# Router search of a mixture-of-experts layer: 6-bit digits and two token chunks per set of mask columns instead of 7-bit digits

## The chip, the cores and the metric

The kernel runs on one core of a Trainium2 chip. The metric is the device time in microseconds (us) of that core. The profile's names for the engines: PE is TensorE (matrix multiply), PEld its weight loads, DVE is VectorE, ACT ScalarE, POOL GpSimd, SP SyncE (which issues most DMA). Engine names with a q are their sequencers.

## The reference

Three stages follow each other: attention with a tanh cap, a dense feed-forward layer with squared ReLU, and a mixture of 8 experts whose assignment is greedy and global:

```
N, D, E, F = 1792, 768, 8, 1024;  cap = N // E          # 224 tokens per expert
logits = x @ w_gate                                      # [1792, 8]
order = argsort(-logits.flatten())                       # best (token, expert) pair first
for idx in order:
    tok, e = idx // E, idx % E
    if assigned[tok] >= 0 or counts[e] >= cap: continue
    assigned[tok] = e; counts[e] += 1
for e in range(E):
    out[assigned == e] = relu(x[assigned == e] @ w1[e]) @ w2[e]
```

Every expert ends with exactly 224 tokens. The kernel doesn't sort. It works in 8 rounds ("routes"). In a round every free token takes its best expert that still has room; the round ends at the logit at which the first expert becomes full; what lies above it is assigned, and that expert is closed.

## The kernel before

**Stages.** Attention of four batches is interleaved with the first layer (`hidden` and `output`, matmuls of 128x128 weights against 448 tokens, each value as a high and a low part, so three matmuls a product: lines 400 to 402 and 457 to 459). From about 600 us on the class method `second` runs two things against each other: the main stream (`output(NB-1)`, `output(LAST)`, then `expert(0)` to `expert(7)`) and the side stream (the last logits, then the routes 0 to 7 and, for each, `listed`, which turns the chosen tokens into row indices for a gather).

**The order of the work.** The order on PE is written by the program (`manual_schedule`). Every step of a stream is a `yield` that adds a planned time to a clock `te`. After each piece of the main stream, a side step is put in as soon as its planned wait is over. These waits are the table `START, MASK, VOTE, REST, GATHER, LIST` (line 45); its first numbers hold until the experts begin, its second ones afterwards (`self.late`). They decide how many main matmuls stand between a route's step on DVE and the matmul that reads its result. PE works strictly in that order: a matmul whose operand isn't ready holds up all behind it. DVE's order comes from a scheduler that ranks route steps and evictions ahead; DVE, too, works in order.

**A route's search.** The 14 token chunks (`TC`) lie as 128 partitions x 14 columns. `m` is each token's best logit and `B` its one-hot expert. The logit's bits are made into a sortable 32-bit key. The threshold at which the first expert is full is searched in digits of `BITS` = 7 bits, so `NDIG` = 5 digits and `NV` = 128 possible values of a digit. A digit works like this:

1. `compare` (L626, DVE): mask[token, value, chunk] = value <= digit of the token, 128x1792 bf16.
2. The vote (L661, PE): for each of the 14 chunks one 128x128 weight load of the mask and one matmul with that chunk's `B` (8 columns), summed in PSUM: how many tokens of each expert lie at or above each value. One more matmul (L662) with a one-row operand takes off the free places (`nroom`).
3. L664 and L665 (DVE): the maximum over the experts, then `>= 0`: P says which values are still full enough.
4. L668 (PE): a matmul of P with ones (`p1`) counts them and spreads the count over all partitions.
5. L671 (DVE): the next digit `D` of every token, from `up` (L657), `p1` and the digits prepared before.

After the digits come the exact ranks: `tm`, then matmuls L682, L684, L689, L690, L703 with DVE steps between, and the rooms are updated. `listed` compares slot numbers with the values 0 to 127 (L738), multiplies (L742, 14 loads and matmuls of 4 columns), and gathers token rows by POOL (L764); `feed` transposes them on PE (L783). The experts' matmuls are L848 (first layer, experts 0 to 3, plain fp32), L855 (experts 4 to 7, split into parts) and L894 (second layer). ACT and DVE split each 128x768 weight tile into its parts (L357, L358), DVE also finishes the evictions of the experts' hidden layer (L866). `finish` transposes an output tile of the layer before (L435) and stores it (L437, L438); the gather of the last two of the six tiles can start only when the last one is stored.

Of the kernel before, what the change touches and what calls it, by code (L numbers as in the profile page):

```python
# [16 lines left out]
OP = mybir.AluOpType  # L17
AX = mybir.AxisListType
# [3 lines left out]
NE, F2 = 8, 1024  # L22
# [22 lines left out]
START, MASK, VOTE, REST, GATHER, LIST = (7.7, 11.0), (2.31, 4.2), (0.9, 3.2), (0.86, 2.6), (11.0, 12.4), (6.0, 16.0)


def shape_constants():
    p = np.arange(128)
    parts, cols = [], {}  # L50

    def add(name, a):
        a = np.asarray(a, np.float32)
        if a.shape[0] < 128:
            a = np.concatenate([a, np.zeros((128 - a.shape[0], a.shape[1]), np.float32)])
        o = sum(x.shape[1] for x in parts)
        cols[name] = (o, o + a.shape[1])
        parts.append(a)

    e = np.arange(NE)  # L60
    add("ident", np.eye(128))
    add("rev", np.tile(8.0 - e, (128, 1)))
    add("first", np.tile(224.0 * e + 1, (128, 1)))
    add("shift", np.tile(BITS * np.arange(NDIG)[::-1], (128, 1)))
    nf = sum(x.shape[1] for x in parts)
    add("tri", p[:, None] < p[None, :])
    c1, e1 = np.divmod(np.arange(TC * NE), NE)
    g2, r2 = np.divmod(np.arange(2 * TC * NE), TC * NE)
    c2, e2 = np.divmod(r2, NE)
    same = e1[:, None] == e2[None]  # L70
    add("above", same * np.where(g2[None] == 0, c1[:, None] < c2[None], True))
    add("tied", same * np.where(g2[None] == 0, False, c1[:, None] < c2[None]))
    add("val", np.tile(np.arange(NV), (128, 1)))
    add("tok", np.stack([np.tile(np.arange(TC), (128, 1)), np.tile(p[:, None], (1, TC))], 2).reshape(128, 2 * TC))
    return np.concatenate(parts, 1), cols, nf

# [4 lines left out]
class Kernel:  # L81
# [485 lines left out]
    def router_setup(self):  # L567
        nc, rp = self.nc, self.rp
        nb = CONSTS.shape[1] - NFC
        tmp = self.wts.tile([128, DM], I64, name="raw", bufs=3).bitcast(F32)[:, :nb]  # L570
        nc.sync.dma_start(tmp, self.cst[:, NFC:])
        self.cb = rp.tile([128, nb], BF, name="cb", bufs=1)
        nc.vector.tensor_copy(self.cb, tmp)
        self.k = lambda n: self.cb[:, COLS[n][0] - NFC:COLS[n][1] - NFC]
        self.tok = self.k("tok").rearrange("p (c k) -> p c k", k=2)
        self.thr = rp.tile([128, NV, TC], BF, name="thr", bufs=1)
        nc.vector.tensor_copy(self.thr, self.k("val")[:, :, None].to_broadcast([128, NV, TC]))
        self.shift = rp.tile([128, NDIG], I32, name="shift", bufs=1)
        nc.vector.tensor_copy(self.shift, self.c("shift"))
        self.unit = rp.tile([128, 2, 128], BF, name="unit", bufs=1)  # L580
        nc.vector.memset(self.unit[:, 0], 1.0)
        nc.vector.memset(self.unit[:, 1], float(NV))
        self.room = rp.tile([128, NE], F32, name="room", bufs=1)
        nc.vector.memset(self.room, float(CAP))
        self.base = rp.tile([128, NE], F32, name="base", bufs=1)
        nc.vector.tensor_copy(self.base, self.c("first"))
        self.todo = rp.tile([128, NE], F32, name="todo", bufs=1)
        nc.vector.memset(self.todo, 1.0)
        self.slot = rp.tile([128, TC], F32, name="slot", bufs=1)
        nc.vector.memset(self.slot, 0.0)  # L590
        self.spacer = rp.tile([1, 1], F32, name="spacer", bufs=1)
        self.full, self.picked, self.rows, self.xe, self.scatters = {}, {}, {}, {}, []
        self.fed = self.gathered = 0
        self.eseq = [(k, m, j) for k in range(NE) for m in (1, 2) for j in range(NF2)]
        self.eloaded = self.eready = self.esplit = 0
        self.ew = {}

    def route(self, k):


        nc, rp, v = self.nc, self.rp, self.nc.vector

        def T(shape, dt, name, bufs=1):
            return rp.tile(shape, dt, name=name, bufs=bufs)
# [7 lines left out]
        v.tensor_reduce(m, self.L, axis=AX.X, op=OP.max)  # L612
        g2 = T([128, 2, TC], F32, "g2")
        B = T([128, TC, NE], BF, "B")

        def choose():
            eo, mx = T([128, TC, NE], F32, "eo"), T([128, TC], F32, "mx")
# [4 lines left out]
            v.tensor_tensor(B, eo, mx[:, :, None].to_broadcast([128, TC, NE]), op=OP.is_equal)  # L622

        def compare(D):
            mask = T([128, NV, TC], BF, "mask")
            v.tensor_tensor(mask, self.thr, D[:, None, :].to_broadcast([128, NV, TC]), op=OP.is_le)  # L626
            return mask

        if k == NE - 1:
            choose()  # L630
            v.memset(g2[:, 0], 1.0)
            v.memset(g2[:, 1], 0.0)
            yield START[self.late], 0.0
        else:
            sg, key = T([128, TC], I32, "sg"), T([128, TC], I32, "key")
            v.tensor_scalar(sg, m.bitcast(I32), 31, -2 ** 31, op0=OP.arith_shift_right, op1=OP.bitwise_or)
            v.tensor_tensor(key, m.bitcast(I32), sg, op=OP.bitwise_xor)
            D0 = T([128, TC], I32, "D0")
            v.tensor_scalar(D0, key, BITS * (NDIG - 1), None, op0=OP.logical_shift_right)
            D = T([128, TC], BF, "D", 2)  # L640
            v.tensor_copy(D, D0)
            mask = compare(D)
            choose()
            nroom = T([1, NE], BF, "nroom")
            v.scalar_tensor_tensor(nroom, self.todo[0:1], 1.0, self.room[0:1], op0=OP.subtract, op1=OP.subtract)
            di, dig = T([128, NDIG, TC], I32, "di"), T([128, NDIG, TC], F32, "dig")
            v.tensor_tensor(di, key[:, None, :].to_broadcast([128, NDIG, TC]),
                            self.shift[:, :, None].to_broadcast([128, NDIG, TC]), op=OP.logical_shift_right)
            v.tensor_scalar(di, di, NV - 1, None, op0=OP.bitwise_and)
            v.tensor_scalar(dig, di, float(NV), None, op0=OP.add)  # L650
            yield START[self.late], 0.0
            for j in range(NDIG):
                if j:
                    mask = compare(D)
                if j < NDIG - 1:
                    up = T([128, TC], F32, "up")
                    v.tensor_scalar(up, D, float(NV), None, op0=OP.mult)  # L657
                yield MASK[self.late], 0.0
                ps = self.psum.tile([NV, NE], F32, name="aux")
                for c in range(TC):  # L660
                    nc.tensor.matmul(ps, mask[:, :, c], B[:, c], start=(c == 0), stop=False)  # L661
                nc.tensor.matmul(ps, self.unit[0:1, 0, :NV], nroom, start=False, stop=True)  # L662
                pm, P = T([NV, 1], F32, "pm"), T([NV, 1], BF, "P")
                v.tensor_reduce(pm, ps, axis=AX.X, op=OP.max)  # L664
                v.tensor_scalar(P, pm, 0.0, None, op0=OP.is_ge)  # L665
                yield VOTE[self.late], 0.4
                p1 = self.psum.tile([128, 1], F32, name="aux")
                nc.tensor.matmul(p1, self.unit[:NV, int(j < NDIG - 1)], P, start=True, stop=True)  # L668
                if j < NDIG - 1:
                    D = T([128, TC], BF, "D", 2)  # L670
                    v.scalar_tensor_tensor(D, up, p1, dig[:, j + 1], op0=OP.subtract, op1=OP.add)  # L671
                else:
                    for g, op in ((0, OP.is_gt), (1, OP.is_equal)):
                        v.tensor_scalar(g2[:, g], D, p1, -1.0, op0=OP.subtract, op1=op)
                yield 0.0, 0.1
        tm = T([128, 2, TC, NE], BF, "tm")
        v.tensor_tensor(tm, B[:, None].to_broadcast([128, 2, TC, NE]),
# [42 lines left out]
    def listed(self, k, es):  # L720

        nc, v = self.nc, self.nc.vector

        def T(shape, dt, name, bufs=1):
            return self.rp.tile(shape, dt, name=name, bufs=bufs)
# [7 lines left out]
        r = T([128, TC], BF, "r")  # L733
        v.scalar_tensor_tensor(r, half[:, :, 1], -float(TP), rel, op0=OP.mult, op1=OP.add)
        v.tensor_tensor(tk, self.tok[:, :, None, :].to_broadcast([128, TC, 2, 2]),
                        half[:, :, :, None].to_broadcast([128, TC, 2, 2]), op=OP.mult)
        oh = T([128, NV, TC], BF, "oh")
        self.picks = v.tensor_tensor(oh, self.thr, r[:, None, :].to_broadcast([128, NV, TC]), op=OP.is_equal)  # L738
        yield LIST[self.late], 0.0
        pi = self.psum.tile([128, 2, 2], F32, name="aux")  # L740
        for c in range(TC):
# [227 lines left out]
```

## Time and profile before

| quantity | value |
|---|---|
| median of 3 runs | 1083.48 us (1083.37 to 1084.87) |
| the profiled execution's own time | 1083.31 us |
| its span | 1081.5 us |
| PE busy | 1054.3 us, 97% of the span |
| DVE, ACT, POOL busy | 594.1 (55%), 470.0 (43%), 247.4 (23%) us |
| votes (35 digits x 14) | 490 matmuls, L661 |

A row of a timeline gives start, duration, engine, line, operation and tiles; where several instructions were merged, the duration is of all and the count stands at the end. Matmuls overlap on PE, so what one costs there is read from the distance between starts, not from its duration.

### The profile page before, as it was taken

Reading aid. Unit: us, or ns where it says so; the run is one execution under the profiler, and the core shown is the slowest. Engines: PE = TensorE matmul, PEld = TensorE weight load, DVE = VectorE, ACT = ScalarE, POOL = GpSimd, SP = SyncE. Lnnn points to the kernel's source line nnn. Section 1 sums busy time; section 2 is a strip of 40 time slices with the busy share of each in tenths; the row PEclk is TensorE's granted clock in tenths of the full one; section 3 lists DMA queues with packets and bytes.
Section 4 is the critical chain, followed back from the end, with each engine's and each line's share of the span. In section 5 each row is a group of like instructions: output and inputs, shape, how many; then the busy total and the mean of one; then the engine's idle time right before and its main releaser. Section 6 shows DMA issues by size and latency. Waiting matters only on the chain.

```text
span 1081.5 us, 15930 instructions
## 1 busy us (share of the span) xinstructions
PE 1054.3 (97%) x5866; PEld 833.7 (77%) x5866; DVE 594.1 (55%) x1066; ACT 470.0 (43%) x725; POOL 247.4 (23%) x181
## 2 busy tenths in 40 slices
PE   6899999999999999999999999999999999999997
PEld 2336656777677677677887888888899999999996
DVE  5997999997222145465411244444546354676550
ACT  5867686544554633454543100002232222454551
POOL 0217684764221322221000100001320201011000
PEclk9999999999999999999999999999999999999999
DMA  8744777899655599987885458567466257556620
GB/s 284 244 139 149 254 265 260 244 325 328 215 182 172 159 301 311 357 290 275 301 301 168 135 171 271 176 191 236 148 238 242 81 182 263 202 195 207 220 78 26
DMA packets 102494, 237.54 MB, mean 220 GB/s; under 512 B 11088, under 2 KB 21872, under 8 KB 102416
## 3 DMA queue, kind: packets, MB, share of 16 engines
q1 hardware_dynamic: 87776, 219.58, 60.4%
q0 software_dynamic: 3424, 11.19, 3.4%
q10 hardware_dynamic: 11216, 5.75, 2.0%
q8 instruction: 46, 0.75, 0.3%
q14 instruction: 32, 0.26, 0.1%
HBM read 194.01 MB, written 42.47 MB: 219 GB/s over the span
## 4 chain that ended last, share of the span: by engine, by line
PE 77%; issue 11%; DVE 6%; DMA 2%; ACT 1%; POOL 1%; SPq 0%; POOLq 0%; DVEq 0%; ACTq 0%
PE acc L457 8%; PE big L894 8%; PE acc L459 7%; PE acc L458 7%; PE acc L400 7%; PE acc L401 6%; PE acc L402 6%; PE acc L848 5%; PE big L234 4%; PE aux L259 4%; PE aux L661 3%; PE acc L855 2%; PE aux L267 2%; DVE wf L330 1%; PE aux L262 1%
## 5 line engine op out<-in xcount | busy, mean ns | idle before, releaser
L457 PE MATMUL acc<-g,wh 128*128 128x448 f32 x384 | 150.6, 392 | 0.0
L400 PE MATMUL acc<-xh,wh 128*128 128x448 f32 x384 | 148.0, 388 | 0.7 <-ACT r L407 0.7
L401 PE MATMUL acc<-xl,wh 128*128 128x448 f32 x384 | 140.9, 367 | 0.8 <-DVE xl L317 0.8
L459 PE MATMUL acc<-g,wl 128*128 128x448 f32 x384 | 139.8, 364 | 0.0
L458 PE MATMUL acc<-g,wh 128*128 128x448 f32 x384 | 139.8, 364 | 0.0
L402 PE MATMUL acc<-xh,wl 128*128 128x448 f32 x384 | 139.8, 364 | 0.0
L894 PE MATMUL big<-wh,g 128*112 128x384 f32 x512 | 118.2, 343 | 0.0
L238 ACT ACTIVATE p<-big,isc 128x896 f32<-128x896 f32 x96 | 85.9, 909 | 43.3 <-PE big L234 39.4
L270 DVE RECIPROCAL z<-z 128x448 f32<-128x448 f32 x24 | 70.7, 2948 | 58.5 <-ACT z L269 58.4
L412 DVE TENSOR_TENSOR g<-r,g 128x448 fp32r<-128x448 f32 x58 | 43.0, 741 | 103.2 <-ACT g L411 102.9
L400 PEld LDWEIGHTS acc<-xh,wh 128*128 128x128 f32 x384 | 71.7, 187 | 34.0 <-issue 14.7
L764 POOL DMA_INDIRECT xg<-x,idx x32 | 34.8, 1087 | 250.1 <-issue 155.0
L239 ACT ACTIVATE p<-p,capt 128x896 f32<-128x896 f32 x96 | 89.4, 948 | 1.5
L894 PEld LDWEIGHTS big<-wh,g 128*112 128x112 f32 x512 | 86.4, 175 | 0.8
L457 PEld LDWEIGHTS acc<-g,wh 128*128 128x128 f32 x384 | 72.4, 189 | 14.3 <-issue 9.6
L234 PE MATMUL big<-qk 64*128 64x448 f32 x288 | 74.5, 601 | 7.0 <-DMA qk<-qk 6.2
L401 PEld LDWEIGHTS acc<-xl,wh 128*128 128x128 f32 x384 | 72.4, 189 | 11.3 <-issue 4.6
L407 ACT ACTIVATE r<-acc 128x448 f32<-128x448 f32 x64 | 34.7, 543 | 100.9 <-PE acc L402 87.6
L402 PEld LDWEIGHTS acc<-xh,wl 128*128 128x128 f32 x384 | 72.2, 188 | 6.8 <-issue 0.8
L459 PEld LDWEIGHTS acc<-g,wl 128*128 128x128 f32 x384 | 72.0, 187 | 6.7 <-issue 0.2
L458 PEld LDWEIGHTS acc<-g,wh 128*128 128x128 f32 x384 | 72.3, 188 | 5.9 <-issue 1.7
L329 DVE TENSOR_SCALAR wf<-raw 128x512 int32<-128x512 int32 (+1 forms) x64 | 49.7, 789 | 48.7 <-DMA raw<-w_out_t 40.1
(179 smaller groups left out, 1865.4 us busy)
## 6 DMA issues: line engine op xcount, KB each, us to landing
g<-w SPq DMA_DIRECT2D x62, 384.0 KB, 6.5
wh<-wih SPq DMA_DIRECT2D x48, 384.0 KB, 4.4
wl<-wil SPq DMA_DIRECT2D x48, 384.0 KB, 4.8
wh<-woh SPq DMA_DIRECT2D x72, 256.0 KB, 2.7
wl<-wol SPq DMA_DIRECT2D x72, 256.0 KB, 3.0
wf<-w SPq DMA_DIRECT2D x33, 384.0 KB, 3.5
raw<-w SPq DMA_DIRECT2D x33, 384.0 KB, 4.3
raw<-w_in SPq DMA_DIRECT2D x16, 768.0 KB, 5.2
```

Source lines behind the costliest of these rows:

```text
L234: nc.tensor.matmul(ps[:, s, :S], k[rows], q[rows], start=True, stop=True)
L238: nc.scalar.activation(p, ps[:, :n, :S], AF.Tanh, scale=self.isc)
L239: e = nc.scalar.activation(p, p, AF.Exp, scale=self.capt)
L270: nc.vector.reciprocal(d, d)
L400: nc.tensor.matmul(ps, wh[:, d], xh, start=(d == 0), stop=False)
L401: nc.tensor.matmul(ps, wh[:, d], xl, start=False, stop=False)
L402: nc.tensor.matmul(ps, wl[:, d], xh, start=False, stop=(d == ND - 1))
L457: nc.tensor.matmul(ps, a, gh, start=(f == 0), stop=False)
L458: nc.tensor.matmul(ps, a, gl, start=False, stop=False)
L459: nc.tensor.matmul(ps, z, gh, start=False, stop=(f == NF - 1))
L848: nc.tensor.matmul(H[j], W[j][0][:, d], xs[:, d, 0].bitcast(F32), start=(d == 0), stop=(d == ND - 1))
L894: nc.tensor.matmul(acc[h][:, s, :DM // 2], l, r[:, s * (DM // 2):(s + 1) * (DM // 2)], start=(j == 0 and first), stop=(j == NF2 - 1 and last))
```

## The change

The digits become 6 bits wide: 6 digits, 64 values. The 128 mask columns of a weight load now hold 64 values for each of two halves of the tokens (`CB` = 2: chunks 0 to 6 and 7 to 13), so that a vote takes 7 matmuls of 16 columns, of which half of each result is used: rows 0 to 63 with the first half's 8 columns, rows 64 to 127 with the second's. The free places (`need`) are now taken off on DVE. Three DVE steps read a vote: `left` = need minus the first half's counts, `ge` = second half's counts >= left, and the maximum over the experts into a vote tile of 128 rows of which the upper 64 stay zero. A chunk row of mask, thresholds and digit is padded from 7 to 8 columns, which makes the mask 128x1024. `slots` takes the place of `thr` in `listed`. Six numbers of the table of waits change.

```
-BITS = 7
+BITS = 6
 NDIG = -(-32 // BITS)
 NV = 2 ** BITS
+CB = 128 // NV
+CP = TC // CB
+CQ = CP + CP % 2
+NS = 128
-START, MASK, VOTE, REST, GATHER, LIST = (7.7, 11.0), (2.31, 4.2), (0.9, 3.2), (0.86, 2.6), (11.0, 12.4), (6.0, 16.0)
+START, MASK, VOTE, REST, GATHER, LIST = (7.7, 8.0), (1.85, 3.4), (1.0, 2.6), (0.86, 2.2), (11.0, 12.4), (6.0, 10.0)
...
+        self.slots = rp.tile([128, NS, TC], BF, name="slots", bufs=1)
+        self.thr = rp.tile([128, CB * NV, CQ], BF, name="thr", bufs=1)
+        self.digit = [rp.tile([128, CB, CQ], BF, name=f"digit{i}", bufs=1) for i in range(2)]
+        self.votes = [rp.tile([128, 1], BF, name=f"votes{i}", bufs=1) for i in range(2)]
+        for d in self.digit + self.votes:
+            nc.vector.memset(d, 0.0)
...
-            mask = T([128, NV, TC], BF, "mask")
-            v.tensor_tensor(mask, self.thr, D[:, None, :].to_broadcast([128, NV, TC]), op=OP.is_le)
+            mask = T([128, CB * NV, CQ], BF, "mask")
+            v.tensor_tensor(mask.rearrange("p (a v) b -> p a v b", a=CB), self.thr.rearrange("p (a v) b -> p a v b", a=CB),
+                            D[:, :, None, :].to_broadcast([128, CB, NV, CQ]), op=OP.is_le)
...
-            nroom = T([1, NE], BF, "nroom")
-            v.scalar_tensor_tensor(nroom, self.todo[0:1], 1.0, self.room[0:1], op0=OP.subtract, op1=OP.subtract)
+            need = T([NV, NE], F32, "need")
+            v.scalar_tensor_tensor(need, self.room[:NV], 1.0, self.todo[:NV], op0=OP.add, op1=OP.subtract)
...
-                ps = self.psum.tile([NV, NE], F32, name="aux")
-                for c in range(TC):
-                    nc.tensor.matmul(ps, mask[:, :, c], B[:, c], start=(c == 0), stop=False)
-                nc.tensor.matmul(ps, self.unit[0:1, 0, :NV], nroom, start=False, stop=True)
-                pm, P = T([NV, 1], F32, "pm"), T([NV, 1], BF, "P")
-                v.tensor_reduce(pm, ps, axis=AX.X, op=OP.max)
-                v.tensor_scalar(P, pm, 0.0, None, op0=OP.is_ge)
-                yield VOTE[self.late], 0.4
+                ps = self.psum.tile([128, CB, NE], F32, name="aux")
+                for c in range(CP):
+                    nc.tensor.matmul(ps, mask[:, :, c], pairs[:, :, c], start=(c == 0), stop=(c == CP - 1))
+                ge, P = T([NV, NE], BF, "ge"), self.votes[j % 2]
+                left = need
+                for a in range(CB - 1):
+                    more = T([NV, NE], F32, f"left{a}")
+                    v.tensor_tensor(more, left, ps[a * NV:(a + 1) * NV, a], op=OP.subtract)
+                    left = more
+                v.tensor_tensor(ge, ps[(CB - 1) * NV:, CB - 1], left, op=OP.is_ge)
+                v.tensor_reduce(P[:NV], ge, axis=AX.X, op=OP.max)
+                yield VOTE[self.late], 0.45
                 p1 = self.psum.tile([128, 1], F32, name="aux")
-                nc.tensor.matmul(p1, self.unit[:NV, int(j < NDIG - 1)], P, start=True, stop=True)
+                nc.tensor.matmul(p1, self.unit[:, int(j < NDIG - 1)], P, start=True, stop=True)
...
-        self.picks = v.tensor_tensor(oh, self.thr, r[:, None, :].to_broadcast([128, NV, TC]), op=OP.is_equal)
+        self.picks = v.tensor_tensor(oh, self.slots, r[:, None, :].to_broadcast([128, NS, TC]), op=OP.is_equal)
```

The matmuls that move stand in the changed order as follows; lines of the changed kernel are 5 to 20 higher (L435 is L440 there, L661 is L677, L668 is L688, L848 is L868, L358 is L363, L783 is L803). Order rows give line, operation, output and inputs; one row of a plain fp32 matmul (L848) stands for two in the profile.

First place: PE while the fifth of the last six output tiles is transposed, in route 3. Before, from one digit's count (L668) to the next vote (L661):

```order
L668 LDWEIGHTS unit
L668 MATMUL aux<-P,unit 128x1
L457 MATMUL acc<-g,wh 128x448
L458 MATMUL acc<-g,wh 128x448
L459 MATMUL acc<-g,wl 128x448
L457 MATMUL acc<-g,wh 128x448
L458 MATMUL acc<-g,wh 128x448
L459 MATMUL acc<-g,wl 128x448
L435 MATMUL aux<-cf,xt 112x128 x4
L661 LDWEIGHTS mask
```

In the changed kernel, in the second digit of route 3:

```order
L688 LDWEIGHTS unit
L688 MATMUL aux<-votes_4841,unit 128x1
L440 MATMUL aux<-cf,xt 112x128 x4
L677 LDWEIGHTS mask
L677 MATMUL aux<-B,mask 128x16
```

Six layer matmuls that stood between the count and the transposes are gone from there; only the four transposes remain between a count and the next vote.

Second place: PE after the transposes of the sixth and last output tile, up to the first transposes of gathered rows (xg). Before, the transposes were followed by one matmul set of `listed` (14 x L742), 12 rows of L848 and a vote, which ends like this:

```order
L662 LDWEIGHTS unit
L662 MATMUL aux<-nroom,unit 128x8
L848 MATMUL big<-xs,raw 128x224 x8
L668 LDWEIGHTS unit
L668 MATMUL aux<-P,unit 128x1
L783 MATMUL aux<-cf,xg_6830 128x112
```

In the changed kernel, from the transposes on:

```order
L440 MATMUL aux<-cf,xt 112x128 x4
L868 MATMUL acc<-xs,wf 128x224 x2
L688 LDWEIGHTS unit
L688 MATMUL aux<-votes_4841,unit 128x1
L868 MATMUL acc<-xs,wf 128x224 x2
L868 MATMUL big<-xs,wf 128x224 x4
L868 MATMUL big<-xs,raw 128x224 x2
L702 LDWEIGHTS cb
L702 MATMUL aux<-tm,cb 128x224
L704 LDWEIGHTS tm
L704 MATMUL aux<-unit,tm 112x1
```

After that stand 6 and 4 more rows of L868 with the route's closing matmuls between them, then the transposes of xg. The L848 rows between the last output transposes and xg are 20 before and 20 now; the vote and the 14 matmuls of `listed` are no longer among them, the closing matmuls of route 3 are.

Third place: DVE in route 4, beside expert 0 (wl is the low part of an expert's weight tile). Before, a digit from its mask to the next:

```order
L626 TENSOR_TENSOR mask<-thr,D 128x1792
L657 TENSOR_SCALAR up<-D 128x14
L664 TENSOR_REDUCE pm<-aux 128x1
L665 TENSOR_SCALAR P<-pm 128x1
L358 TENSOR_TENSOR wl<-wf,wh 128x768 x2
L671 SCALAR_TENSOR_TENSOR D<-up,aux,dig 128x14
L358 TENSOR_TENSOR wl<-wf,wh 128x768
```

In the changed kernel:

```order
L641 TENSOR_TENSOR mask<-thr,digit_4839 128x1024
L673 TENSOR_SCALAR up<-digit_4839 128x14
L363 TENSOR_TENSOR wl<-wf,wh 128x768
L682 TENSOR_TENSOR left_7001<-need,aux 64x8
L363 TENSOR_TENSOR wl<-wf,wh 128x768
L684 TENSOR_TENSOR ge<-aux,left_7001 64x8
L363 TENSOR_TENSOR wl<-wf,wh 128x768
L685 TENSOR_REDUCE votes_4841<-ge 64x1
L363 TENSOR_TENSOR wl<-raw,wh 128x768
L691 SCALAR_TENSOR_TENSOR digit_4838<-up,aux,dig 128x2x7
```

The weight splits now stand between the three steps that read the vote, ahead of the last of them too.

## Rows read from the trace of the kernel before

**Rows 1.** The page: span, and busy time of each engine.

```profile
span 1081.5 us, 15930 instructions
PE 1054.3 (97%) x5866; PEld 833.7 (77%) x5866; DVE 594.1 (55%) x1066; ACT 470.0 (43%) x725; POOL 247.4 (23%) x181
```

**Rows 2.** The page: the chain that ended last, shares by engine.

```profile
PE 77%; issue 11%; DVE 6%; DMA 2%; ACT 1%; POOL 1%; SPq 0%; POOLq 0%; DVEq 0%; ACTq 0%
```

**Rows 3.** Waits of PE from 590 us on: total, times, longest.

```profile
PE aux L783 <- DMA xg<-x,idx: 1.4, 1, 1.4
PE acc L848 <- DVE g L866: 0.9, 2, 0.5
PE acc L855 <- DVE g L866: 0.6, 2, 0.4
PE acc L848 <- ACT xs L788: 0.6, 1, 0.6
```

**Rows 4.** Timeline, one digit of route 0: start, duration, engine, line, operation.

```profile
625.58 0.36 PE L459 MATMUL acc<-g,wl 128*128 128x448 f32 x1
625.78 1.00 PE L661 MATMUL aux<-B,mask 128*128 128x8 bf16 x14
626.72 0.17 PE L662 MATMUL aux<-nroom,unit 1*128 1x8 bf16 x1
626.82 0.47 PE L457 MATMUL acc<-g,wh 128*128 128x448 f32 x1
626.93 0.17 DVE L664 TENSOR_REDUCE pm<-aux 128x1 f32<-128x8 f32 x1 [2.02 <-PE aux L662]
627.13 0.16 DVE L665 TENSOR_SCALAR P<-pm 128x1 bf16<-128x1 f32 x1
627.13 0.37 PE L458 MATMUL acc<-g,wh 128*128 128x448 f32 x1
...
628.15 0.18 PE L668 MATMUL aux<-P,unit 128*128 128x1 bf16 x1
628.19 0.45 PE L457 MATMUL acc<-g,wh 128*128 128x448 f32 x1
...
628.48 0.36 PE L458 MATMUL acc<-g,wh 128*128 128x448 f32 x1
...
628.66 1.09 DVE L626 TENSOR_TENSOR mask<-thr,D 128x1792 bf16<-128x1792 bf16 x1
```

**Rows 5.** Groups from 600 us on: count, busy us, mean ns, idle before.

```profile
L661 PEld LDWEIGHTS <-mask 128*128 128x128 bf16 x490 | 32.9, 157 | 5.3 <-issue 4.7 <-DVE up L657 0.2
L742 PEld LDWEIGHTS <-oh 128*128 128x128 bf16 x112 | 7.5, 158 | 1.1 <-DVE B L622 0.7 <-issue 0.3
L668 PE MATMUL aux<-P,unit 128*128 128x1 bf16 x35 | 6.1, 174 | 0.0
L894 PEld LDWEIGHTS big<-wl,g 128*112 128x112 f32 x256 | 44.0, 174 | 0.3
L358 DVE TENSOR_TENSOR wl<-wf,wh 128x768 fp32r<-128x768 f32 x24 | 23.0, 958 | 20.1 <-ACT wh L357 20.0
L697 DVE TENSOR_TENSOR A<-aux,room 128x224 bf16<-128x224 f32 x8 | 3.1, 387 | 5.3 <-PE aux L690 5.3
```

**Rows 6.** Timeline, the four transposes between a vote and its count.

```profile
672.66 0.65 PE L435 MATMUL aux<-cf,xt 128*112 128x128 f32 x4
673.18 0.16 PE L668 MATMUL aux<-P,unit 128*128 128x1 bf16 x1
```

**Rows 7.** Timeline, the last output tile: transposes, store, gather, transposes of gathered rows.

```profile
759.08 0.60 PE L435 MATMUL aux<-cf,xt 128*112 128x128 f32 x4
...
760.34 0.31 ACTq L438 DMA_DIRECT2D x<-rows  x1
...
765.94 3.29 PE L848 MATMUL big<-xs,raw 128*128 128x224 f32 x16
...
766.86 0.92 POOL L764 DMA_INDIRECT xg<-x,idx  x1 [0.30 <-issue]
...
769.07 0.17 PE L668 MATMUL aux<-P,unit 128*128 128x1 bf16 x1
...
770.76 0.51 PE L783 MATMUL aux<-cf,xg 112*128 112x112 f32 x3 [1.37 <-DMA xg<-x,idx]
```

**Rows 8.** Windows after it: busy us (count) PE, PEld, DVE, ACT, POOL; clock; DMA.

```profile
774.00:775.00 1.00, 1.00 (x3) 0.92 (x4) 0.38 (x3) 0.00 (x0) 0.00 (x0) 0.50 0.77 227
776.00:777.00 1.00, 1.00 (x4) 0.89 (x4) 0.39 (x1) 0.68 (x2) 0.00 (x0) 0.55 0.33 68
```

More of the change, by code (lines that the diff above doesn't have):

```diff
@@ L72, in shape_constants @@
     add("tied", same * np.where(g2[None] == 0, False, c1[:, None] < c2[None]))
-    add("val", np.tile(np.arange(NV), (128, 1)))
+    add("val", np.tile(np.arange(NS), (128, 1)))
+    add("low", np.tile(np.arange(NS) % NV, (128, 1)))
     add("tok", np.stack([np.tile(np.arange(TC), (128, 1)), np.tile(p[:, None], (1, TC))], 2).reshape(128, 2 * TC))
@@ L575, in router_setup @@
         self.tok = self.k("tok").rearrange("p (c k) -> p c k", k=2)
-        self.thr = rp.tile([128, NV, TC], BF, name="thr", bufs=1)
-        nc.vector.tensor_copy(self.thr, self.k("val")[:, :, None].to_broadcast([128, NV, TC]))
+        self.slots = rp.tile([128, NS, TC], BF, name="slots", bufs=1)
+        nc.vector.tensor_copy(self.slots, self.k("val")[:, :, None].to_broadcast([128, NS, TC]))
+        self.thr = rp.tile([128, CB * NV, CQ], BF, name="thr", bufs=1)
+        nc.vector.tensor_copy(self.thr, self.k("low")[:, :, None].to_broadcast([128, CB * NV, CQ]))
+        self.digit = [rp.tile([128, CB, CQ], BF, name=f"digit{i}", bufs=1) for i in range(2)]
+        self.votes = [rp.tile([128, 1], BF, name=f"votes{i}", bufs=1) for i in range(2)]
+        for d in self.digit + self.votes:
+            nc.vector.memset(d, 0.0)
         self.shift = rp.tile([128, NDIG], I32, name="shift", bufs=1)
@@ L614, in route, with chunks @@
         B = T([128, TC, NE], BF, "B")
+        pairs = B.rearrange("p (a b) e -> p a b e", a=CB)
+        def chunks(x):
+            return x.rearrange("p (a b) -> p a b", a=CB)
         def choose():
@@ L639, in route @@
             v.tensor_scalar(D0, key, BITS * (NDIG - 1), None, op0=OP.logical_shift_right)
-            D = T([128, TC], BF, "D", 2)
-            v.tensor_copy(D, D0)
+            D = self.digit[0]
+            v.tensor_copy(D[:, :, :CP], chunks(D0))
             mask = compare(D)
             choose()
-            nroom = T([1, NE], BF, "nroom")
-            v.scalar_tensor_tensor(nroom, self.todo[0:1], 1.0, self.room[0:1], op0=OP.subtract, op1=OP.subtract)
+            need = T([NV, NE], F32, "need")
+            v.scalar_tensor_tensor(need, self.room[:NV], 1.0, self.todo[:NV], op0=OP.add, op1=OP.subtract)
             di, dig = T([128, NDIG, TC], I32, "di"), T([128, NDIG, TC], F32, "dig")
@@ L656, in route @@
                     up = T([128, TC], F32, "up")
-                    v.tensor_scalar(up, D, float(NV), None, op0=OP.mult)
+                    v.tensor_scalar(chunks(up), D[:, :, :CP], float(NV), None, op0=OP.mult)
                 yield MASK[self.late], 0.0
-                ps = self.psum.tile([NV, NE], F32, name="aux")
-                for c in range(TC):
-                    nc.tensor.matmul(ps, mask[:, :, c], B[:, c], start=(c == 0), stop=False)
-                nc.tensor.matmul(ps, self.unit[0:1, 0, :NV], nroom, start=False, stop=True)
@@ L669, in route @@
                 if j < NDIG - 1:
-                    D = T([128, TC], BF, "D", 2)
-                    v.scalar_tensor_tensor(D, up, p1, dig[:, j + 1], op0=OP.subtract, op1=OP.add)
+                    D = self.digit[(j + 1) % 2]
+                    v.scalar_tensor_tensor(D[:, :, :CP], chunks(up), p1, chunks(dig[:, j + 1]), op0=OP.subtract, op1=OP.add)
                 else:
                     for g, op in ((0, OP.is_gt), (1, OP.is_equal)):
-                        v.tensor_scalar(g2[:, g], D, p1, -1.0, op0=OP.subtract, op1=op)
+                        v.tensor_scalar(chunks(g2[:, g]), D[:, :, :CP], p1, -1.0, op0=OP.subtract, op1=op)
@@ L736, in listed @@
                         half[:, :, :, None].to_broadcast([128, TC, 2, 2]), op=OP.mult)
-        oh = T([128, NV, TC], BF, "oh")
-        self.picks = v.tensor_tensor(oh, self.thr, r[:, None, :].to_broadcast([128, NV, TC]), op=OP.is_equal)
+        oh = T([128, NS, TC], BF, "oh")
+        self.picks = v.tensor_tensor(oh, self.slots, r[:, None, :].to_broadcast([128, NS, TC]), op=OP.is_equal)
         yield LIST[self.late], 0.0
```

## The prediction

> **What bounds the kernel now.** I read the page first. PE is busy for 1054.3 of 1081.5 us [rows 1], and the chain that ended last runs over PE for 77% of the span, with another 11% of "issue", against 6% for DVE [rows 2]. So time goes away only if PE gets less to do or waits less. Second, PE's own waits in the stretch where the router works: 3.5 us in four groups, the largest the 1.4 us for the gathered rows xg [rows 3]. No wait for a router step stands among them: the planned waits leave room, and the router is hidden except for what its matmuls cost on PE. Third, the timeline of one digit shows that cost [rows 4], and the grouped lines give its parts over all digits [rows 5].
>
> **What a digit costs PE before.** Layer matmuls start 0.20 us apart (625.58 to 625.78, where the vote follows) [rows 4]. The 14 mask loads keep the load path busy for 32.9 us over 490, 67 ns each [rows 5], so 0.94 us a vote (625.78 to 626.72, the same). The one-row matmul for the free places adds 0.10 (to 626.82). The first layer matmul after it lasts 0.31 instead of 0.20 until its successor starts (627.13): 0.11 for the return. The count adds 0.04 (628.15 to 628.19) and a return of 0.09 (0.29 instead of 0.20, 628.48): 0.13. Sum 0.94 + 0.10 + 0.11 + 0.13 = 1.28 us, 35 times (35 counts, [rows 5]).
>
> **What a digit costs after.** Seven loads and matmuls instead of 14: 7 x 0.067 = 0.47, no one-row matmul, the same returns: 0.47 + 0.11 + 0.13 = 0.71 us, 42 times. I take 0.067 us for the new matmul although it has 16 columns instead of 8 and its weight columns lie 16 bytes apart instead of 28. The matmuls of `listed` have 4 columns, the same 28 bytes, and need the same 67 ns (7.5 us over 112) [rows 5], so the columns don't set the distance at this size. No row shows the 16-byte step. The bounds: nothing gained or lost per load, 67 ns, and at the other end loads that no longer overlap, 157 ns, the mean duration of one [rows 5]. The nearest row is the mask load itself; I take 67.
>
> The Trainium skill ("SBUF — State Buffer", section "Door 1: The DMA port swizzle", on cachelines) says that accesses which move to a new 16-byte line pay a penalty. A step of 28 bytes takes a new line for each weight as well, so by that rule the load costs as much as before; its price could have been higher only against packed columns. No run shows the new step yet.
>
> **Which of it counts.** One stretch of PE is bound by DMA, not by PE: from the transposes of the last output tile (759.08) over its store (760.34) and the second gather (766.86) to the arrival of its rows (770.76) [rows 7]. These 11.7 us stay, whatever PE does in them. Before, one vote with its count and one set of `listed` stood there for nothing; now one count and the closing matmuls of route 3 do, by the order of the program, beside the same 20 rows of L848. So I count 34 digits before: 34 x 1.28 = 43.5. After: 42 votes x 0.58 and 41 counts x 0.13 = 24.4 + 5.3 = 29.7. A set of `listed` comes back onto the path, 14 x 0.067 + 0.11 = 1.05, and six closing matmuls go from it, 6 x 0.067 and three returns of 0.11 = 0.7. Saved: 43.5 - 29.7 - 1.05 + 0.7 = 13.4 us.
>
> **What the change adds.**
>
> - *Three DVE steps instead of two between vote and count.* Dependent small steps start 0.20 us apart (626.93 to 627.13) [rows 4]: P is ready 0.2 us later, some 0.8 us after the vote. Each step is between 0.16 us (L665, [rows 4]) and 0.39 (L697, 224 columns out of PSUM, [rows 5]); 8 columns are nearer to the first. In the layer phase six layer matmuls and a return stand between vote and count: 626.82 to 628.15, 1.33 us [rows 4]. That covers it, so it costs nothing there. Where only the four transposes stand in between, the count came 0.52 us after them before [rows 6]; the changed order has this once in the layer phase (route 1, last digit), and there PE waits about 0.3 to 0.4.
> - *A smaller mask.* 1792 columns take 1.09 us, a step of one column 0.16 [rows 4], so 0.52 ns a column and 0.16 + 1023 x 0.52 ns = 0.69 us for 1024. If the padded four-level pattern ran at half that rate it would be 1.22. From a count to a ready mask: 0.51 us (628.15 to 628.66) [rows 4] + 0.69 + 0.1 = 1.3 us. Twelve layer matmuls cover 2.4 us. In the second digit of route 3 only the four transposes are left between a count and the next vote (first place of the order), 0.52 us [rows 6]: PE waits 0.8 us, or 1.3 with the slow mask.
> - *Shorter planned waits beside the experts.* There a vote is followed by 12 matmuls of L894 at 0.174 us [rows 5], 2.1 us, or by 6 rows of L848, twelve matmuls at 0.195 (16 in 765.94 to 769.07, [rows 7]), 2.3 us. Without other work P needs 0.8. But DVE is in order, and in route 4 two weight splits of 0.96 us (L358, [rows 5]) stand before the last of the three steps (third place of the order): 0.8 + 1.9 = 2.7 us against some 2.75 with the transposes in that gap. Behind a waiting count stands everything on PE. A split itself waits for ACT's cast, and that for its weight tile, so a late tile is now handed on to PE at once. The floor is 0 (all covered), the ceiling one split of 0.96 for each of some 18 digits beside the experts; the order shows such a split in about a third of them, mostly with cover. I take 1.2 us in all.
> - *More idle at the last store.* In the fixed 11.7 us PE has about 1.3 us less to do, which is no loss by itself. But after the 1.4 us of waiting the granted clock stood at 0.50 and 0.55 in two windows (1.2 of 2.4 GHz) [rows 8]; a longer idle time can hold it there longer. Two more such windows would cost 1 us; I take 0.7.
> - *The rest* is hidden: the setup copies of the new tables on DVE come well before the first mask, and DVE's own sum for a digit hardly moves, three steps and 0.69 against two and 1.09.
>
> The Trainium skill ("TensorE: Matmul & The Clock Gate", section "What's actually happening") says that the gate falls to half after idle time and rises after sustained work. The trace agrees as far as it goes, with 0.50 behind this wait [rows 8]; how far a longer idle moves it, no run shows.
>
> **The sum.** 0.35 + 0.8 + 1.2 + 0.7 = 3.05 us added, 13.4 saved, 10.3 net: 1083.31 - 10.3 = 1073.0 us. The sum is made against the profiled execution, 1083.31 us, whose span of 1081.5 leaves 1.8 around it; that run lies 0.17 under the median of the runs shown.
>
> **Rivals.**
>
> 1. *Hardly any new wait.* The splits and casts run ahead of need, DVE always has P in time, and the clock drop keeps its length: 13.4 less about 1.2 for the two bare places, 1071. For it: PE waited for no router step before. Against it: the waits in the table are cut together with a longer DVE chain.
> 2. *Counts stuck behind weight splits.* If the order's two splits fall into most votes beside the experts, each of some 18 is late by 0.5 us (2.7 against 2.1 to 2.3): 9 us, and 1083.3 - 13.4 + 1.2 + 9 = 1080. For it: the third place of the order, and split groups that wait 20.0 us for ACT [rows 5]. Against it: most digits in that order have one split or none.
> 3. *Slower: mask loads that no longer overlap.* The 16-byte step makes each load and matmul take 157 ns: 294 x 0.090 = 26.5 us more, 1083.3 - 10.3 + 26.5 = 1099.5. It is slower than before from 0.067 + 10.3 / 294 = 0.102 us a matmul on. For it: no row has this step. Against it: the two kinds of strided loads that the rows have, with 4 and with 8 columns, both come to 67 ns [rows 5].
> 4. *The change doesn't do what it says:* the votes were hidden, as at the last store. Then the time stays at 1083. Against it: a layer matmul stands directly on both sides of every vote [rows 4].
>
> **How the numbers follow.** Forecast (1071.8 to 1076) 0.58, rival 1 (1069.5 to 1071.8) 0.17, rival 2 (1076 to 1081) 0.17, rival 3 0.04, rival 4 0.02, anything else 0.02. The range 1069.5 to 1078.5 holds the first two and half of the third, about 0.83. Below 0.2% (2.2 us) a measurement of this kernel can't be told from no change: faster 0.93, same 0.03, slower 0.04.
>
> **What would show it.** In the changed profile: 294 mask loads with some 20 us of load time; 0.47 us from a vote's first matmul to the matmul behind it; no one-row matmul; a mask of 0.7 us; one bare place of 0.8 us in route 3; the xg transposes still 11.7 us after the last output transposes, with more idle before them; waits of the count for the vote steps of about 1 us in total beside the experts. Wrong would be: a distance of mask matmuls above 0.1 us, or waits of PE for L685's result above 4 us, or waits of the experts' matmuls for weights that weren't there before.

## The result and the profile after

Over six runs each the changed kernel takes 1073.03 us (1070.67 to 1076.87) and the kernel before 1083.72 (1082.83 to 1084.87): ratio 0.9899, 95% interval 0.9887 to 0.9911. Forecast were 1073.0 us. The profiled execution took 1072.59 us. The six lie in the order of their mean granted clock, from 1070.67 us at 0.997 of full speed to 1076.87 at 0.990; the profiled executions of both kernels had 0.995.

The page of the changed kernel, with the lines that answer to [rows 1, 2]:

```profile
span 1070.8 us, 15562 instructions
PE 1038.1 (97%) x5642; PEld 817.0 (76%) x5642; DVE 601.2 (56%) x1148; ACT 470.3 (44%) x725; POOL 247.2 (23%) x181
PE 75%; issue 10%; DVE 7%; DMA 4%; ACT 2%; POOL 1%; SPq 0%; POOLq 0%; DVEq 0%; ACTq 0%
```

PE works 16.2 us less, but the span is only 10.7 us shorter: PE now waits more. PE's waits from 590 us on (total, times, longest), against [rows 3]:

```profile
PE aux L688 <- DVE votes L685: 3.5, 4, 2.4
PE acc L868 <- DVE g L886: 2.5, 1, 2.5
PE aux L803 <- DMA xg<-x,idx: 0.8, 1, 0.8
...
PE aux L677 <- DVE mask L641: 0.6, 1, 0.6
```

The first and the last group are the router's own steps, for which PE never waited before.

One digit of route 0 (start, duration, engine, line, operation), against [rows 4]:

```profile
623.89 0.37 PE L464 MATMUL acc<-g,wl 128*128 128x448 f32 x1
624.10 0.59 PE L677 MATMUL aux<-B,mask 128*128 128x16 bf16 x7
624.55 0.45 PE L462 MATMUL acc<-g,wh 128*128 128x448 f32 x1
624.73 0.15 DVE L682 TENSOR_TENSOR left<-need,aux 64x8 f32<-64x8 f32 x1 [1.92 <-PE aux L677]
624.84 0.36 PE L463 MATMUL acc<-g,wh 128*128 128x448 f32 x1
624.92 0.17 DVE L684 TENSOR_TENSOR ge<-aux,left 64x8 bf16<-64x8 f32 x1
...
625.12 0.15 DVE L685 TENSOR_REDUCE votes<-ge 64x1 bf16<-64x8 bf16 x1
...
625.86 0.18 PE L688 MATMUL aux<-votes,unit 128*128 128x1 bf16 x1
625.89 0.45 PE L462 MATMUL acc<-g,wh 128*128 128x448 f32 x1
```

A vote takes 0.45 us to the next layer matmul, and that one 0.29 instead of 0.20. P is ready at 625.27, 0.72 us after the vote, and the count follows at 625.86: here the third DVE step is covered.

The groups from 590 us on (count, busy us, mean ns, idle before), against [rows 5]:

```profile
L641 DVE TENSOR_TENSOR mask<-thr,digit 128x1024 bf16<-128x1024 bf16 x42 | 28.9, 689 | 1.1
L677 PEld LDWEIGHTS <-mask 128*128 128x128 bf16 x294 | 22.4, 161 | 6.4 <-issue 4.9 <-DVE mask L641 0.8 <-DVE wl L363 0.2
L762 PEld LDWEIGHTS <-oh 128*128 128x128 bf16 x112 | 7.6, 160 | 1.0 <-issue 0.8 <-DVE tm L697 0.2
```

The mask takes the 0.69 us that was estimated. The busy time of the mask loads divided by their number is 76 ns (22.4 / 294), against 67 before. That isn't the price of the 16-byte step: a set is seven loads now and was 14, and the start of each set counts in its busy time. With each vote doubled (below), 588 loads with the 16-byte step come to 68 ns each, as much as those of `listed` with 28 bytes (7.6 / 112).

The longest count wait, in the fourth digit of route 3 (timeline; in brackets the idle time and what ended it):

```profile
734.75 5.46 SPq L835 DMA_DIRECT2D g<-w  x6
...
743.24 0.83 ACT L362 CAST wh<-g 128x768 fp32r<-128x768 f32 x1 [5.28 <-DMA x<-rows]
...
744.11 0.96 DVE L363 TENSOR_TENSOR wl<-g,wh 128x768 fp32r<-128x768 f32 x1 [3.14 <-ACT wh L362]
...
744.99 0.15 DVE L682 TENSOR_TENSOR left<-need,aux 64x8 f32<-64x8 f32 x1
745.19 0.96 DVE L363 TENSOR_TENSOR wl<-g,wh 128x768 fp32r<-128x768 f32 x1
...
746.18 0.17 DVE L684 TENSOR_TENSOR ge<-aux,left 64x8 bf16<-64x8 f32 x1
746.38 0.16 DVE L685 TENSOR_REDUCE votes<-ge 64x1 bf16<-64x8 bf16 x1
746.59 0.16 PE L688 MATMUL aux<-votes,unit 128*128 128x1 bf16 x1 [2.42 <-DVE votes L685]
```

The first weight tiles of expert 0 are asked for at 734.75. ACT casts them, DVE's first split waits for that cast, and `left`, `ge` and the maximum stand behind two splits in DVE's order. PE stands still for 2.42 us. Behind it, a window (busy time and count of PE, PEld, DVE, ACT, POOL; then the clock):

```profile
747.00:748.00 1.00, 1.00 (x6) 0.96 (x5) 0.81 (x3) 0.93 (x2) 0.00 (x0) 0.50 0.00 0
```

The granted clock is 0.50 (1.2 of 2.4 GHz). Summed over windows of 1 us, the clock that is missing from 746 to 750 is worth 1.7 us, as much as before from 773 to 777 [rows 8], where it is whole now. The stall has moved the drop, not added one.

The last output tile's store, gather and transposes, against [rows 7]:

```profile
753.89 0.62 PE L440 MATMUL aux<-cf,xt 128*112 128x128 f32 x4
...
755.17 0.31 ACTq L443 DMA_DIRECT2D x<-rows  x1
...
758.45 0.92 POOL L784 DMA_INDIRECT xg<-x,idx  x1 [5.35 <-DMA x<-rows]
...
763.70 0.51 PE L803 MATMUL aux<-cf,xg 112*128 112x112 f32 x3 [0.84 <-DMA xg<-x,idx]
```

The stretch is 9.8 us long, not 11.7. From the store's issue to its landing the list of transfers has 2.5 us, against 4.5 before. Before, a gather of other rows was still in transfer beside the store; now the first gathers are issued at 750.95 and 752.18, before it.

A second new stall stands at 888.17 (same kind of rows):

```profile
881.12 0.14 DVE L736 TENSOR_SCALAR ei<-es 1x1 int32<-1x1 f32 x1
...
883.45 0.83 ACT L362 CAST wh<-wf 128x768 fp32r<-128x768 f32 x1 [1.95 <-DMA wf<-w]
...
884.31 0.96 DVE L363 TENSOR_TENSOR wl<-wf,wh 128x768 fp32r<-128x768 f32 x1 [1.63 <-ACT wh L362]
...
888.17 2.16 PE L868 MATMUL acc<-xs,raw 128*128 128x224 f32 x10 [2.52 <-DVE g L886]
```

The router's choice of an expert (`ei`) lets its weights load; DVE idles 1.63 us for the cast of the first, and the eviction `g` behind that comes late for PE. Before, the like cost 0.50 [rows 3].

### The profile page after: what moved, and what is told of

It reads as the page before. It is cut to its first block, busy times and chain, and to the rows that moved or that the text cites. A ratio compares the mean times of both kernels' runs of the same rounds, so it can differ in the third digit from the quotient of the medians.

```text
span 1070.8 us, 15562 instructions
## 1 busy us (share of the span) xinstructions
PE 1038.1 (97%) x5642; PEld 817.0 (76%) x5642; DVE 601.2 (56%) x1148; ACT 470.3 (44%) x725; POOL 247.2 (23%) x181
## 4 chain that ended last, share of the span: by engine, by line
PE 75%; issue 10%; DVE 7%; DMA 4%; ACT 2%; POOL 1%; SPq 0%; POOLq 0%; DVEq 0%; ACTq 0%
PE acc L462 8%; PE acc L463 7%; PE acc L464 7%; PE big L914 7%; PE acc L405 7%; PE acc L406 6%; PE acc L407 6%; PE acc L868 5%; PE big L239 4%; PE aux L264 4%; PE acc L875 3%; PE aux L272 2%; DMA raw<-w 2%; DVE wf L335 1%; PE aux L267 1%
## 5 line engine op out<-in xcount | busy, mean ns | idle before, releaser
L784 POOL DMA_INDIRECT xg<-x,idx x32 | 31.1, 971 | 278.4 <-issue 182.1
L363 POOL TENSOR_TENSOR wl<-wf,wh 128x512 fp32r<-128x512 f32 (+1 forms) x33 | 57.8, 1757 | 74.3 <-ACT wh L362 71.5
```

The source lines that it names most:

```text
L363: low.tensor_sub(wl[:, :w], wf[:, :w], wh[:, :w].bitcast(F32))
```

## Experiments

All were timed against the kernel before on their own chip (medians 1083.96 to 1084.49 us).

**The table of waits on the new digits.**

```
-START, MASK, VOTE, REST, GATHER, LIST = (7.7, 8.0), (1.85, 3.4), (1.0, 2.6), (0.86, 2.2), (11.0, 12.4), (6.0, 10.0)
+START, MASK, VOTE, REST, GATHER, LIST = (7.7, 11.0), (2.31, 4.2), (0.9, 3.2), (0.86, 2.6), (11.0, 12.4), (6.0, 16.0)
```

> The changed kernel with the old table of planned waits (START 11.0, MASK 4.2, VOTE 3.2, REST 2.6, LIST 16.0 beside the experts). Theory (the gain comes from PE work that is gone; the table is only there so that six digits a route still end in time): by its order on PE the closing matmuls of routes 6 and 7, the list and the transposes of gathered rows then stand next to each other with no expert work between; PE has to sit through some 20 us of DVE steps and a gather there, against 3.5 us of count waits saved. 1085 to 1095 us. Rival (the table doesn't matter): 1073, within 2.

Measured: 1103.46 us (1100.43 to 1104.91), ratio 1.0174 (1.016 to 1.0189). PE's largest waits:

```profile
PE acc L803 <- DMA xg<-x,idx: 9.0, 2, 5.5
PE aux L702 <- DVE tm L697: 5.6, 2, 5.2
```

Six digits with the old waits end too late. From 995 to 1018 us PE sits through the closing steps of route 7 and its gather, 20 us of waiting in all, as the theory said. The time lies 8 us above its range: behind these waits the clock stands at half from 997 to 1024 us, which the theory had not counted. (SP, too, waits 62 us for the choice of route 7's expert, but PE then waits for none of its weights.) So the shorter waits are a part of the change that it can't do without.

**The table alone, on the kernel before** (the same line the other way round).

> The kernel before with the new table of planned waits and nothing else: 490 mask matmuls as before. Theory: the same work on PE, no waits there to shorten, one or two bare places more with a mask of 1.09 us: 1083 to 1086 us. Rival (the shorter waits bring the gain): 1075 to 1078.

Measured: 1088.78 us (1086.78 to 1095.04), ratio 1.0041 (1.0026 to 1.0055). PE's waits:

```profile
PE aux L661 <- DVE mask L626: 2.0, 2, 1.0
```

Two votes of 7-bit digits wait 1.0 us each for the larger mask. That is the bare place that was expected, but not the whole loss, and the time lies above the range. In the profiled execution, the slowest of the six (1095.04 us), the clock that is missing ahead of the end of the program is worth 8.5 us, in three places, against 1.7 in the kernel before. So the table loses by itself some 4 us; the gain comes from the rest of the change.

**Each vote twice**, to see whether votes are on PE's path.

```
-                for c in range(CP):
+                for _ in range(2):
+                    for c in range(CP):
```

> The changed kernel with each vote's seven loads and matmuls done twice (the second set starts the sum anew, so the result is the same). Theory (each load and matmul of a vote costs 0.067 us on the path): 294 x 0.067 = 19.7 us more, 1091 to 1094 us. Rival (votes are hidden beside waits): under 5 us more, 1073 to 1078.

Measured: 1089.53 us (1087.63 to 1090.53), ratio 1.0049 (1.0036 to 1.0063), 16.5 over the changed kernel and a little below the theory's range. A vote, then the loads and the count waits:

```profile
624.63 1.03 PE L678 MATMUL aux<-B,mask 128*128 128x16 bf16 x14
625.51 0.45 PE L462 MATMUL acc<-g,wh 128*128 128x448 f32 x1
```

```profile
L678 PEld LDWEIGHTS <-mask 128*128 128x128 bf16 x588 | 40.2, 163 | 6.3 <-issue 4.5 <-DVE mask L641 0.8 <-DVE B L637 0.4
PE aux L689 <- DVE votes L686: 0.7, 3, 0.4
```

A vote now takes 0.88 us to the next layer matmul instead of 0.45, so 42 votes 18 us more, and a load that is added 61 ns ((40.2 - 22.4) / 294). PE's waits take back 1.3 us: the counts wait 0.7 us instead of 3.5, but evictions 4.6 instead of 2.9. So votes count in full on PE's path.

**The free places on DVE alone, in the kernel before** (7-bit digits; the one-row matmul goes, DVE keeps two steps).

```
-                nc.tensor.matmul(ps, self.unit[0:1, 0, :NV], nroom, start=False, stop=True)
...
+                v.tensor_tensor(ge, ps, need, op=OP.is_ge)
+                v.tensor_reduce(P, ge, axis=AX.X, op=OP.max)
```

> The kernel before with one part of the change alone: the free places are compared on DVE (counts >= need, then the maximum; two steps as before) and the one-row matmul of each vote is gone. Theory: 34 votes on the path at 0.10 us: 3.4 us less, 1080.3 us, 0.9969 of the kernel before. Rival (the one-row matmul is hidden in the pipeline): no change, within 1 us.

Measured: 1077.31 us (1076.13 to 1078.43), ratio 0.9935 (0.992 to 0.9949): 7.1 us, twice what was expected. One vote in its timeline:

```profile
622.17 0.37 PE L459 MATMUL acc<-g,wl 128*128 128x448 f32 x1
622.38 1.01 PE L661 MATMUL aux<-B,mask 128*128 128x8 bf16 x14
623.25 0.45 PE L457 MATMUL acc<-g,wh 128*128 128x448 f32 x1
...
623.53 0.36 PE L458 MATMUL acc<-g,wh 128*128 128x448 f32 x1
```

From vote to next layer matmul 0.87 us, where [rows 4] have 0.94 + 0.10. Over the 14 votes between layer matmuls, a vote with its return costs 0.96 us here and 1.16 before: the one-row matmul is 0.20 us, half of it shown as a later end of the 14 before it and a longer return. 34 x 0.20 = 6.8 us. In this execution, besides, the clock doesn't fall behind the xg transposes (1.7 us were missing there before) and the stretch of the last store is 10.5 us instead of 11.7; the three together would be more than was measured, so how the 7.1 us divide is not settled.

This is the run to remember: 7.1 of the 10.7 us come with a part of the change that needs no narrower digits. What the 6-bit digits, with their table, add to it is about 4 us (1077.31 against 1073.03; ratios 0.9935 and 0.9899).

**The count over 64 rows**, so that the vote tile is not padded.

```
-                nc.tensor.matmul(p1, self.unit[:, int(j < NDIG - 1)], P, start=True, stop=True)
+                nc.tensor.matmul(p1, self.unit[:NV, int(j < NDIG - 1)], P[:NV], start=True, stop=True)
```

> The changed kernel with the count as a matmul over 64 rows of the vote tile and of the ones instead of the 128 padded rows. Theory (a count costs its switch, whatever the rows): no change, within 1.5 us of 1073. Rival (a change of the row count makes PE empty its pipeline around each count): 0.1 to 0.2 us for each of 42 counts, 1077 to 1081.

Measured: 1081.83 us (1078.09 to 1083.76), ratio 0.997 (0.9956 to 0.9983), 8.8 over the changed kernel, or 7.7 by the two ratios; the rival was right. A count in its timeline:

```profile
621.14 0.37 PE L464 MATMUL acc<-g,wl 128*128 128x448 f32 x1
621.44 0.17 PE L688 MATMUL aux<-votes,unit 64*128 64x1 bf16 x1
621.55 0.47 PE L462 MATMUL acc<-g,wh 128*128 128x448 f32 x1
621.86 0.36 PE L463 MATMUL acc<-g,wh 128*128 128x448 f32 x1
```

The distances are 0.30, 0.11 and 0.31, with 128 rows 0.21, 0.03 and 0.29 (starts at 625.65, 625.86, 625.89 and 626.18; the middle two stand above): 0.19 us more, 42 times 8 us. It is nearly the price of the one-row matmul. The Trainium skill ("TensorEngine Tiling (Array Packing)", section "Key Properties") says that a change of the tiling mode, to which the number of rows belongs, drains TensorE. The two runs agree with that, at 0.2 us each time; the page gives no figure.

**No padding of the chunk rows** (mask 128x896, a step of 14 bytes).

```
-CQ = CP + CP % 2
+CQ = CP
```

> The changed kernel without the padding of a chunk row from 7 to 8 columns (mask 128x896 instead of 128x1024, weight columns 14 bytes apart). Theory: the mask gets slower per column, about 1.1 us instead of 0.69, since rows of odd length can't be taken in pairs, but twelve layer matmuls cover it; only the bare place in route 3 and perhaps a few votes beside the experts wait 0.4 us more: 1073 to 1076 us. The loads keep 0.067 to 0.076 us. Rival 1 (the mask bounds a digit): 42 x 0.4 = 17 us more, 1090. Rival 2 (the padding buys nothing): mask 0.6 us and 1072.

Measured: 1073.22 us (1071.09 to 1074.51), ratio 0.989 (0.9873 to 0.9906), not to be told from the changed kernel. The groups:

```profile
L641 DVE TENSOR_TENSOR mask<-thr,digit 128x896 bf16<-128x896 bf16 x42 | 28.9, 689 | 1.1
L677 PEld LDWEIGHTS <-mask 128*128 128x128 bf16 x294 | 19.9, 149 | 6.6 <-issue 4.5 <-DVE mask L641 0.8 <-DVE B L637 0.3
```

The time fell into the theory's range, but its reason failed: 896 columns take DVE 0.69 us, not 1.1, as long as 1024, so the padding is free there and buys nothing. In sets of seven, as in the changed kernel, the loads come to 68 ns instead of 76, and a vote to 0.39 us instead of 0.45: 42 x 0.06 = 2.5 us less. In the profiled execution, the slowest of the five, the count wait is 0.6 longer (3.04), and the clock that is missing is worth 5.1 us instead of 1.7 (the end of the program aside), behind that wait and once more at 889. There this gives the 2.5 us back. The Trainium skill ("SBUF — State Buffer", section "Door 1: The DMA port swizzle") has a penalty for each access that moves to a new 16-byte line. By that rule steps of 28 and 16 bytes cost the same, and 14 bytes a little less, since one weight in eight stays in its line. The runs agree: 67 and 68 ns in sets of 14, and 68 instead of 76 in sets of seven. That the line is the reason, no run shows.

**Splits on POOL.** The low parts of the first 12 expert tiles are computed by POOL.

```
-            self.ew[self.eloaded] = (wf,) if plain else (wf, DM, nc.vector, pool, bufs)
+            self.ew[self.eloaded] = (wf,) if plain else (wf, DM, nc.gpsimd if self.eloaded < NF2 + 4 else nc.vector, pool, bufs)
```

> The changed kernel with the low parts of the first split weight tiles of expert 0 (the first 12 of the load sequence that are split) computed on POOL instead of DVE; the order on PE is unchanged. Theory: the 2.4 us wait of a count in route 3, where a weight split on DVE stands between the vote and its three steps and waits for its tile's DMA, goes away, and with it the half clock that followed (about 1.3 us): 3 to 4 us less, 1069 to 1070.5 us. Rival (the wait belongs to the vote's own chain, or the next split takes its place): 1073, within 1.

Measured: 1076.49 us (1075.98 to 1081.64), ratio 0.9929 (0.9916 to 0.9942), slower than the changed kernel; the profiled execution is the slowest of the six. Its timeline:

```profile
746.04 5.84 POOL L363 TENSOR_TENSOR wl<-g,wh 128x768 fp32r<-128x768 f32 x3 [9.47 <-ACT wh L362]
746.45 1.46 DVE L691 SCALAR_TENSOR_TENSOR digit<-up,aux,dig 128x14 bf16<-128x14 f32 x1 [0.81 <-PE aux L688]
747.95 2.25 DVE L641 TENSOR_TENSOR mask<-thr,digit 128x1024 bf16<-128x1024 bf16 x1
...
750.26 0.60 PE L677 MATMUL aux<-B,mask 128*128 128x16 bf16 x7 [2.18 <-DVE mask L641]
```

The count's wait is gone, which shows the splits as its cause. But while POOL works, the digit step takes 1.46 us instead of 0.24 and the mask 2.25 instead of 0.69, and votes wait for the mask. The Trainium skill ("SBUF — State Buffer", section "SBUF: two separate sides") has GpSimd and VectorE, in its 2-port modes or with two SBUF inputs, lock a shared pair of ports for a whole instruction; the stretched steps beside POOL's, which both read two tiles in SBUF, agree.

**Splits after route 3**, held back in DVE's order.

```
...
-            with self.tc.issue_after(self.picks.ins) if self.eready < 2 * NF2 else nullcontext():
+            with self.tc.issue_after(self.searched.ins) if self.eready < 2 * NF2 else nullcontext():
```

> The changed kernel; the splits of expert 0's second-layer weight tiles (ACT and DVE) may start only behind marks in route 3's closing steps on DVE, not beside its last three digits. PE's order is unchanged and no work goes to POOL. Theory: the 2.4 us wait of the count in route 3 and the half clock after it (1.3 us) go, and nothing slows DVE: 1069 to 1070.5 us, 0.986 to 0.988 of the kernel before. Rival 1 (the splits are then late for expert 0's second layer, with 11 us of DVE work packed into less time): 1073 or more. Rival 2 (the wait comes from the vote's own three steps): 1073.

Measured: 1074.29 us (1072.5 to 1076.26), ratio 0.9912 (0.9897 to 0.9926), not to be told from the changed kernel. A wait later on, in its timeline:

```profile
775.09 0.55 PE L677 MATMUL aux<-B,mask 128*128 128x16 bf16 x7 [3.00 <-DVE B L637]
```

PE hardly waits for counts any more (0.2 us), and the transposes of xg come at 760.04 instead of 763.70. But the splits now delay `B` of route 4, and its first vote waits 3.00 us, with half the clock behind it. Rival 1 was right in its mechanism.

**The same, with route 4 starting later, and then without padding too** (e10, e11).

```
-            yield START[self.late], 0.0
+            yield 11.5 if k == 4 else START[self.late], 0.0
```

> e9_splits_after_route with one wait longer: route 4 starts its search 11.5 us of planned time after its preparation instead of 8.0, so that 20 instead of 4 matmuls of L914 (0.174 us each, so 2.8 us more) stand between the listing of route 3 and the first vote of route 4. Theory (a wait on PE counts in full, and the 2.42 us of the changed kernel and the 3.00 us of e9 are the same excess of DVE work met at two places): with both covered the time falls by about the 3.0 us and the half clock behind it (1.3 us) against e9, 1074.3 - 4.3 = 1070 us; no PE wait above 1 us between 590 and 880 us. Rival 1 (the wait moves on once more, to a later vote of route 4 or to the experts' evictions): 1073 to 1075. Rival 2 (the later search makes a later expert's choice late, as with the old waits): above 1076, with a new wait of PE or SP after 850 us.

> e10_later_first_vote with chunk rows of 7 instead of 8 columns (mask 128x896). Theory: the mask loads go from 76 to 68 ns as in e6_no_pad, 294 x 0.008 = 2.4 us less load time; in e6 a longer count wait (3.04 instead of 2.42) hid part of it, here that wait is gone, so about 1 to 2.4 us under e10_later_first_vote. Rival (the loads' time lies beside other work of PE, the padding is worth nothing): the same as e10 within 0.8 us.

Measured: 1071.78 us (1070.96 to 1072.78), ratio 0.9887 (0.987 to 0.9903), and 1071.58 (1070.41 to 1071.72), 0.9884 (0.9867 to 0.99). Timeline of the first, PE's largest waits:

```profile
774.30 0.60 PE L914 MATMUL big<-wh,g 128*112 128x384 f32 x2 [1.37 <-DVE g L886]
...
882.07 8.76 PE L868 MATMUL acc<-xs,raw 128*128 128x224 f32 x36 [1.91 <-DVE g L886]
```

No vote or count waits over 0.6 us any more, but evictions of the experts now wait. Summed, PE's waits outside the stretch of the last store are 8.0 us, against 7.4 in the changed kernel. The medians are 1.3 and 1.5 us better, the intervals overlap with the changed kernel's: neither is shown to beat it. Of the first, rival 1 comes nearest in its mechanism (the wait moved on, to evictions) and the theory in its time; of the second the rival holds in its time, 0.2 us, but not in its reason: the loads take 19.9 us instead of 22.5, and in its profiled execution the clock that is missing is worth 3.4 us instead of 1.7.

## Why the prediction was right

By its terms, in us, from the two profiled executions (digits as the mean of 14 votes that stand between layer matmuls):

| term | predicted | measured |
|---|---|---|
| a digit before | 1.28 | 1.16 + 0.14 = 1.29 |
| a digit after | 0.71 | 0.55 + 0.14 = 0.69 |
| saved by digits, `listed` and closing | 13.4 | 34 x 1.29 - 42 x 0.55 - 41 x 0.14 - 0.35 = 14.7 |
| stretch of the last store | 0 | 11.7 - 9.8 = 1.9 saved |
| new waits outside it | 0.35 + 0.8 + 1.2 = 2.35 | 7.4 - 1.5 = 5.9 |
| longer half clock | 0.7 | 0 |
| net | 10.3 | 10.7 (spans: 10.7) |

- *Digits.* Right, and the largest term. A load costs what it did (68 against 67 ns in sets of 14), and a vote of seven took 0.45 us, not 0.47; the return after it is 0.09, not 0.11. Inside the digit before, 0.10 for the one-row matmul was half of its price (the free-places run); the sum was read from distances and held it anyway. But the prediction looked for the gain in the mask loads, and 34 x 0.20 = 6.8 of these 14.7 us are the one-row matmul.
- *Bare places.* 0.16 for the count in route 1 (0.35 predicted), 0.59 for the vote in route 3 (0.8). Right in place and nearly in size.
- *Waits beside the experts.* Counts wait 0.62 and 0.34 us there, 0.96 in sum against 1.2. Right. But the step stopped at the experts' beginning: the same mechanism, a weight split that waits for a cast ahead of a vote's DVE steps, struck 2.42 us in route 3. The weight loads now start 19 us before the last output transposes, 14 before (issued at 745.43, transposes in [rows 7]); that this brought the splits there was not tested. This term was mis-sized by its place.
- *The eviction at 888* (2.52, before 0.50) was not predicted at all. It stands in the kernel with the old waits too (2.39 at 882) and not in the one with the new waits and old digits (0.3 in all for this group), so it comes with the digits, not with the table; what exactly shifts it was not tried.
- *The fixed 11.7 us* was the step that failed: it became 9.8, with a shorter store and less idle before the xg transposes, not more. That the store was slowed by gathers beside it before is read from the transfers and was not tested.
- *Half clock.* As much as before, at another place. 0.7 was too much.

So the mechanism was right, but that the time came out to 0.1 us is luck: 1.3 us for the digits, 1.9 for the stretch and 0.7 for the clock were taken too low, and 3.5 us of waits were missing. The executions themselves lie 6 us apart. Rival 2 (1080) was the nearest in kind; the doubled votes rule out rival 4, and the 0.45 us of a vote rival 3.

## What to carry to other kernels

Price small matmuls between large ones by distances of starts over the whole digit, and keep their row count that of their neighbours: a single 64-row or one-row matmul cost 0.2 us, and dropping the one-row matmul alone gave two thirds of this change's gain. Compare load times only between sets of the same length. Where several streams share an in-order engine, a saved microsecond shifts transfers against steps, and the engine's queue brings part of it back as a wait elsewhere; moving the work behind that wait (splits after the route, on POOL) mostly moved the wait. A table of planned waits is tuned for one length of the steps: the new table lost 4 us with the old digits, and the old one 30 us with the new.

## What the runs showed of the hardware

- One 64-row matmul among 128-row ones costs 0.19 us more than one of 128 rows, a one-row matmul 0.20 us in all; part shows as a later end of the matmuls before it.
- A 128x896 comparison in bf16 with rows of 7 takes the 689 ns of 128x1024 with rows of 8.
- Mask loads in sets of 14 take 67 ns each with a 28-byte step and 68 with 16; in sets of seven 76 with 16 and 68 with 14.
- DVE steps took 1.46 and 2.25 us instead of 0.24 and 0.69 beside elementwise work of POOL.
